# Soft-MoE attention on one core: six-pair logits blocks, a longer warm-up and small fill products in the last chain

## The chip, the cores and the metric

The kernel runs on one core of a Trainium2 chip. The metric is device time of one execution in microseconds (us), as the median of three runs. A profiled execution gives, beside its own time, a trace of each engine: TensorE (PE, with its weight loads PEld), VectorE (DVE), ScalarE (ACT), GpSimd (POOL) and the queue of SyncE (SP), which issues all DMAs of this kernel.

## What is computed

Attention with a sigmoid in place of the softmax is followed by a mixture of experts with soft routing (8 experts, 4 slots each), all in fp32:

```python
scores = scale * q @ k.T - log(S)            # 8 batches, 12 heads, S = 448, head size 64
x = sigmoid(scores) @ v                      # then x: 3584 x 768
logits = x @ phi                             # 3584 x 32
d = softmax(logits over the 3584 tokens)     # slot_input = d.T @ x : 32 x 768
h = relu(slot_input[e] @ w1[e])              # per expert, F = 1024
slot_out[e] = h @ w2[e]
c = softmax(logits over the 32 slots)
out = c @ slot_out                           # 3584 x 768
```

## The kernel before

Two heads make a pair (128 partitions), six pairs a batch, 48 pairs in all. The attention runs in 24 iterations `n` of the loop at L427, two pairs (`pa`, `pb`) each, so three iterations make a batch. The order of the instructions on PE, SP, DVE and ACT is written out by hand; every engine works through its own list in order and waits by semaphore. In an iteration PE runs `qk_full` of both pairs (L176), `av_full` of `pa` and of `pb` (L195), then `qk_mid` for the next iteration (L187) and `av_mid` (L204). DVE copies the sums of an iteration out of PSUM at the beginning of the next (`evac`, L213) into a tile `x0` or `x1`, in turn.

The logits of a pair are four products with 32 output columns (`logits_job`, L224), each into a column group of its own: with fp32, eight instructions for a pair. Before the change every iteration from the second on computes the logits of the two pairs of the iteration before it, 16 instructions in PSUM, and `logits_add` copies or adds them into `lt_all` on DVE. In the first iteration of a batch (`edge`) this stands between the two `av_full` and completes the batch before; the softmax over the tokens follows it on DVE and ACT. In the second (`after`) `spread` sends the softmax weights through DRAM: one DMA out (`zd`, L292) and four back (`dr`, L295), and `slot_mm` (L318) multiplies them with the transposed x (`y`); its products come in four groups `a` for each block `c` of 32 tokens, four products of two instructions each in a group, and group `a` reads partitions 32a and up, and so what the a-th of the four DMAs brings.

The last iteration (L461 to L479) has no next one: the partial logits of the last batch in `lt_all` are put back in PSUM by a product with the identity (L465), the pairs that are missing are added, and `last_job` does the softmax with the maximum over tokens and the slot sums in one chain. In its pauses `warm(2)` (L355) runs products nobody reads.

Weights come as 128 units of 384 KB: 64 of w1, 64 of w2. The first 50 (`N_A`) go to tiles `wa` of their own during the attention. Then, behind the last loads of v in SP's list, 18 (`N_B`) go to tiles `wb`, which lie where the attention's tiles lay: each waits until the tiles under it are free. In order of address these are the q/k tiles and their splits, `v0`, `att4`, `x0`, `att3`, `v2`, `att0` to `att2`, `v1`, a gap, `y` with `dr`, and `x1`. `wb` 0 to 14 end where `y` begins; the last three lie over `y` and wait for the last `slot_mm`. All later units and the output tiles go round the ring of these 68 tiles, each when its last reader is done: w1 products (L535), w2 products (L601), output products (L578) and their copies (L583), stores (L592).

At the start, while q and k come in, 37 small products (32x32 weights, 8 columns, L415) and three large ones (128x128, L417) run on a zeroed tile `acc`; `qk_mid(0)` follows.

Of the kernel before, what the change touches and what calls it, by code (L numbers as in the profile page):

```python
# [9 lines left out]
F32 = mybir.dt.float32  # L10
# [14 lines left out]
NFC = F // P  # L25
HALF = DM // 2
UNIT = 768
GAP = 128
N_A = 50
N_B = 18  # L30
N_LATE = 16
N_MIX = 4
QW = 2 * S
NP = B * NPR
NG = B * NQ
WARM = 3
FILL = 37
WN = 128
CW = 256
NBK = 4  # L40
# [8 lines left out]
def soft_moe_attention(ctx: ExitStack, tc: tile.TileContext, qk, v, phi, w1, w2, cst, out):  # L49
# [16 lines left out]
    acc = small.tile([P, DM], F32, name="acc")  # L66
    phi_t = small.tile([P, 256], F32, name="phit")
    phi_sb = phi_t[:, 0:NKC * NSLOT].rearrange("p (k s) -> p k s", k=NKC)
    nc.vector.memset(acc[:, 0:256], 0.0)
    nc.vector.memset(nbias, -math.log(S))  # L70
    nc.gpsimd.memset(lt_all, NEG)

    units = [("w1", e, 2 * uu + y, kh) for e in range(E) for uu in range(2) for kh in range(2) for y in range(2)]
    units += [("w2", hf, e, g, y) for hf in range(2) for e in range(E) for g in range(2) for y in range(2)]
# [42 lines left out]
    with ExitStack() as actx:  # L117
        ldq = actx.enter_context(tc.tile_pool(name="ldq", bufs=2))
        sp = actx.enter_context(tc.tile_pool(name="sp", bufs=2))
        one = {}  # L120
        for name in ("v0", "att4", "x0", "att3", "v2", "att0", "att1", "att2", "v1", "gap"):
            one[name] = actx.enter_context(tc.tile_pool(name=f"{name}p", bufs=1))
        yp = actx.enter_context(tc.tile_pool(name="yp", bufs=1))
        one["x1"] = actx.enter_context(tc.tile_pool(name="x1p", bufs=1))
        one["gap"].tile([P, GAP], F32, name="gap")
        bounce = actx.enter_context(tc.tile_pool(name="bounce", bufs=2, space=bass.MemoryType.DRAM))
        ps = actx.enter_context(tc.tile_pool(name="ps", bufs=1, space=PSUM))

        def bank2(i):
            return ps.tile([P, 2, 512], F32, name=f"b{i}")  # L130
# [73 lines left out]
                    nc.tensor.matmul(avs["p", 2 * n + i][d, 0:S], vt[r, 0, d], att[r, h, :], start=start, stop=stop)  # L204

        def new_x(n):
            xTs[n] = one[f"x{n % 2}"].tile([P, 2, S], F32, name=f"x{n % 2}")
            for i in range(2):
                xTs["p", 2 * n + i] = xTs[n][:, i, :]

# [10 lines left out]
        def logits_job(lp, pairs, first=True, last=True):  # L221
            for m, p in enumerate(pairs):
                for j in reversed(range(4)):
                    nc.tensor.matmul(  # L224
                        lp[32 * j:32 * j + 32, 0:TOK[j]], phi_sb[:, p % NPR, :],
                        xTs["p", p][:, TOF[j]:TOF[j] + TOK[j]],
                        start=(first and m == 0), stop=(last and m == len(pairs) - 1))

        def logits_add(lp, b, first):
            for r, w in ((slice(0, 64), TOK[0]), (slice(64, 128), TOK[3])):  # L230
                dst, part = lt_all[r, b, 0:w], lp[r, 0:w]
                if first:
                    nc.vector.tensor_copy(dst, part)
                else:
                    nc.vector.tensor_tensor(out=dst, in0=part, in1=dst, op=ALU.add)

        def logits(n, i):
            lp = bank2(i)[:, 0, :]
            logits_job(lp, (2 * n, 2 * n + 1))
            return lp  # L240

        def softmax_a(b):
            t1 = small.tile([P, 2, 132], F32, name="t1")
# [100 lines left out]
        def last_job(b, lg):  # L344
            t1 = small.tile([P, 2, 132], F32, name="t1")
            pe = t1[:, 0, 0:P]
            sw, sw2 = t1[:, 1, 0:NSLOT], t1[:, 1, 64:64 + NSLOT]
            m1 = small.tile([P, 2], F32, name="m1")
            cw = small.tile([P, 8], F32, name="cw")
            pa = bank2(1)  # L350
            pw = bank2(3)[:, 0, :]

            def warm(n):
                for _ in range(n):
                    nc.tensor.matmul(pw[:, 0:P], ident, ident, start=True, stop=True)  # L355

            nc.vector.tensor_reduce(out=m1[:, 0:1], in_=lg, axis=AX.X, op=ALU.max)
            nc.vector.tensor_scalar(cw[:, 0:1], m1[:, 0:1], mz[:, 0:1], -1.0, op0=ALU.max, op1=ALU.mult)
            nc.vector.tensor_tensor(out=m1[:, 1:2], in0=m1[:, 0:1], in1=mz[:, 0:1], op=ALU.max)
            nc.scalar.activation(pe, lg, AF.Exp, bias=cw[:, 0:1])  # L360
            nc.scalar.activation(cw[:, 1:2], mz[:, 0:1], AF.Exp, bias=cw[:, 0:1])
            warm(2)
            nc.tensor.matmul(pa[0:1, 0, 0:P], m1[:, 1:2], ident, start=True, stop=True)
            warm(2)
            pr = fan_out(b, pe)
            mrow = small.tile([1, 1, NSLOT], F32, name="mrow")
            nc.vector.tensor_reduce(
                out=mrow[:], in_=pa[0:1, 0, 0:P].rearrange("o (j s) -> o s j", j=4), axis=AX.X, op=ALU.max)
            fan_in(b, pr)
            for j in range(4):  # L370
                nc.tensor.matmul(pa[32 * j:32 * j + 32, 1, 0:1], mrow[:, 0, :], csb[0:1, 0:1], start=True, stop=True)
            sl = slot_mm(b, (2, 3))
            nc.vector.tensor_tensor(out=cw[:, 2:3], in0=m1[:, 1:2], in1=pa[:, 1, 0:1], op=ALU.subtract)
            nc.scalar.activation(cw[:, 3:4], cw[:, 2:3], AF.Exp)
            nc.vector.tensor_scalar(sw, sel4, cw[:, 3:4], None, op0=ALU.mult)
            nc.vector.tensor_scalar(sw2, sw, cw[:, 1:2], None, op0=ALU.mult)
            fresh = xTs[NG - 1].rearrange("p z n -> p (z n)")[:, 0:DM]
            for g, copy in enumerate((nc.scalar.copy, nc.vector.tensor_copy)):
                copy(fresh.rearrange("p (g a x) -> p g a x", g=2, a=2)[:, g], new_of(sl, g))
            pt = bank2(1)[:, 0, 0:NKC * BLK]  # L380
            for i, (part, w) in enumerate(((acc, sw2), (fresh, sw))):
                for a in range(4):
                    nc.tensor.matmul(  # L383
                        pt[32 * a:32 * a + 32, :], w, part[:, a * NKC * BLK:(a + 1) * NKC * BLK],
                        start=(i == 0), stop=(i == 1))
            nc.vector.transpose(sT[:].rearrange("p k s -> p (k s)"), pt)  # L386
            nc.scalar.copy(lt_all[:, b], lg)
            nc.vector.tensor_reduce(out=cw[:, 4:5], in_=pe, axis=AX.X, op=ALU.add)
            nc.vector.scalar_tensor_tensor(
                out=cw[:, 5:6], in0=mz[:, 1:2], scalar=cw[:, 1:2], in1=cw[:, 4:5], op0=ALU.mult, op1=ALU.add)  # L390
            nc.vector.tensor_tensor(out=cw[:, 6:7], in0=cw[:, 5:6], in1=cw[:, 3:4], op=ALU.mult)


            def finish(pool):
                pz = pool.tile([P, 2, 512], F32, name="px")[:, 0, :]
                nc.tensor.matmul(pz[:, 0:1], rep, cw[:, 6:7], start=True, stop=True)
                nc.vector.tensor_scalar(rz[:], pz[:, 0:1], 1e-9, None, op0=ALU.add)
                nc.vector.reciprocal(rz[:], rz[:])

            return finish  # L400
# [9 lines left out]
        nc.sync.dma_start(csb[:], cst)  # L410
        nc.sync.dma_start(phi_sb, phi)
        pw = bank2(0)[:, 0, :]
        for i in range(FILL):
            r = slice(i % 4 * 32, i % 4 * 32 + 32)
            nc.tensor.matmul(pw[r, 0:8], acc[r, 0:32], acc[r, 0:8], start=True, stop=True)  # L415
        for _ in range(WARM):
            nc.tensor.matmul(pw[:, 0:WN], acc[:, 0:P], acc[:, 0:WN], start=True, stop=True)  # L417
        dmy = one["att2"].tile([P, 2, S], F32, name="att2")
# [8 lines left out]
        for n in range(NG):  # L427
# [33 lines left out]
            if final:  # L461
                avs["p", pa] = bank2(2)[:, 0, :]
                av_full(pa, True, False)
                lg = bank2(0)[:, 0, 0:P]
                nc.tensor.matmul(lg, ident, lt_all[:, B - 1], start=True, stop=False)  # L465
                logits_job(lg, [NP - 4, NP - 3], first=False, last=False)
                avs["p", pb] = bank2(3)[:, 0, :]
                av_mid(n, ((False, True), (True, False)))
                new_x(n)
                xa, xb = xTs["p", pa], xTs["p", pb]  # L470
                nc.vector.tensor_copy(xa, avs["p", pa][:, 0:S])
                turn(pa)
                av_full(pb, False, True)
                logits_job(lg, [pa], first=False, last=False)
                nc.scalar.copy(xb[:, 256:S], avs["p", pb][:, 256:S])
                nc.vector.tensor_copy(xb[:, 0:256], avs["p", pb][:, 0:256])
                logits_job(lg, [pb], first=False)
                turn(pb)
                break  # L479
# [2 lines left out]
                avs["p", pa + i] = avs[n][:, i, :]  # L482
            av_full(pa, True, False)
            if edge:
                lp = logits(n - 1, 3)
                logits_add(lp, bp, False)
                softmax_a(bp)
                softmax_b(bp)
            av_full(pb, True, False)
            if n > 0 and not edge:  # L490
                lp = logits(n - 1, 3 if after else 0)
                if after:
                    combine_b(bp)
                logits_add(lp, n // NQ, n % NQ == 1)
            if after:
                slot_job(bp)
            qk_mid(n + 1)
# [96 lines left out]
    def warm(n):  # L594
        for _ in range(n):
            nc.tensor.matmul(wt[:, 0:P], ident, ident, start=True, stop=True)
# [82 lines left out]
```

## Time and profile before

| | us |
|---|---|
| median of 3 runs (lowest, highest) | 392.69 (391.61, 393.25) |
| the profiled execution | 390.81 |
| its span, first to last instruction | 389.0 |
| PE busy in the span | 364.2 |
| DVE, ACT, POOL busy | 226.5, 190.2, 3.3 |
| DMA | 97.54 MB, mean 251 GB/s |

The profile gives start and duration of each instruction, and for idle time the event that ended it. fp32 products appear as two instructions each. The span is cut here at about 284 us: before, it is attention, and after, weights and output. The profiled execution is 1.88 us below the median of the runs.

### The profile page before, as it was taken

How to read it: one execution, taken by the hardware profiler on the slowest of the kernel's cores; microseconds unless marked ns; L12 is line 12 of the kernel's file. 1: busy time of each engine (PE TensorE's matmuls, PEld its weight loads, DVE VectorE, ACT ScalarE, POOL GpSimd, SP SyncE). 2: the span in 40 equal slices, each digit the busy share in tenths (PEclk: the TensorE clock that was granted, in tenths of full speed). 3: DMA queues.
4: the chain of work that ended last, by engine and by line, in shares of the span. 5: the costliest groups of instructions: out<-in, count | busy, mean ns of one | idle time of the engine just before them, and what ended most of it. 6: DMA issues, size and time to landing. Idle time of an engine off the chain costs nothing.

```text
span 389.0 us, 9831 instructions
## 1 busy us (share of the span) xinstructions
PE 364.2 (94%) x4058; PEld 188.8 (49%) x4058; DVE 226.5 (58%) x518; ACT 190.2 (49%) x243; POOL 3.3 (1%) x13
## 2 busy tenths in 40 slices
PE   8999999999999999999999999999989989977750
PEld 5444556554555654555554456555455543313210
DVE  3555776776887677697667777776643410420340
ACT  4656675664667456566645666564530110320240
POOL 1000000000000000000000000000020000000000
PEclk9999999999999999999999999999999999999995
DMA  7777856773784567477547755442899999999987
GB/s 212 256 245 238 285 156 192 244 255 102 244 296 144 183 227 239 161 240 244 195 137 227 274 159 203 142 150 70 294 390 387 401 399 402 383 385 374 366 287 242
DMA packets 49276, 97.54 MB, mean 251 GB/s; under 512 B 5584, under 2 KB 26704, under 8 KB 49232
## 3 DMA queue, kind: packets, MB, share of 16 engines
q1 hardware_dynamic: 49232, 96.92, 72.7%
q8 instruction: 32, 0.52, 0.6%
q14 instruction: 12, 0.10, 0.1%
HBM read 85.43 MB, written 11.47 MB: 249 GB/s over the span
## 4 chain that ended last, share of the span: by engine, by line
PE 85%; DMA 9%; DVE 2%; ACT 1%; issue 1%; SPq 0%; ACTq 0%
PE b L195 29%; PE b L176 24%; PE b L187 6%; PE px L535 6%; PE b L204 5%; DMA wb<-in_w_dram 4%; PE b L318 4%; DMA wa<-in_w_dram 3%; PE b L224 3%; PE po L601 3%; PE px L578 2%; PE px L552 1%; DMA qkt<-in_qk_dram 1%; DVE wa L583 1%; PE b L383 0%
## 5 line engine op out<-in xcount | busy, mean ns | idle before, releaser
L164 ACT ACTIVATE att<-b,nbias 128x896 f32<-128x896 f32 x168 | 158.6, 1007 | 84.7 <-PE b L187 64.7
L195 PE MATMUL b<-att,v 128*64 128x448 f32 x576 | 115.3, 545 | 0.0
L176 PE MATMUL b<-qs,ks 64*128 64x448 f32 x864 | 95.7, 372 | 0.0
L176 PEld LDWEIGHTS b<-qs,ks 64*128 64x128 f32 x864 | 77.4, 184 | 26.3 <-PE b L187 6.3
L195 PEld LDWEIGHTS b<-att,v 128*64 128x64 f32 x576 | 38.5, 136 | 61.6 <-issue 54.1
L213 DVE COPY x<-b 128x896 f32<-128x896 f32 x23 | 25.1, 1091 | 33.1 <-PE b L204 33.1
L155 DVE TENSOR_TENSOR qs<-qkt,qs 128x448 fp32r<-128x448 f32 x48 | 30.0, 625 | 1.7
L155 DVE TENSOR_TENSOR ks<-qkt,ks 128x384 fp32r<-128x384 f32 x48 | 26.8, 558 | 1.6
L219 DVE STREAM_TRANSPOSE y<-x 128x448 f32<-128x448 f32 x48 | 27.3, 617 | 0.4
L187 PE MATMUL b<-qkt 64*64 64x448 f32 x192 | 25.2, 569 | 0.3 <-DMA qkt<-in_qk_dram 0.2
L153 DVE CAST qs<-qkt 128x448 fp32r<-128x448 f32 x48 | 18.4, 384 | 9.6 <-DMA qkt<-in_qk_dram 6.5
L204 PE MATMUL b<-att,v 64*64 64x448 f32 x192 | 22.4, 537 | 0.0
L583 DVE COPY wa<-px 96x768 f32<-96x768 f32 x13 | 12.2, 952 | 13.2 <-PE px L578 13.2
L583 ACT COPY wa<-px 128x768 f32<-128x768 f32 x13 | 10.3, 799 | 17.6 <-PE px L578 14.2
L535 PE MATMUL px<-wa,sT 128*32 128x256 f32 x300 | 17.8, 381 | 0.6 <-DVE sT L386 0.6
L578 PE MATMUL px<-st,lt_all 32*128 32x384 f32 (+1 forms) x128 | 16.8, 524 | 1.5 <-DVE st L614 0.7
L318 PE MATMUL b<-y,dr 32*32 32x192 f32 x896 | 17.7, 331 | 0.2 <-ACT dr L309 0.2
L224 PEld LDWEIGHTS b<-x,phit 128*32 128x32 f32 x384 | 9.1, 109 | 17.0 <-issue 11.3
L153 DVE CAST ks<-qkt 128x384 fp32r<-128x384 f32 x47 | 16.6, 353 | 0.0
L224 PE MATMUL b<-x,phit 128*32 128x96 f32 (+1 forms) x384 | 16.0, 266 | 0.2
L614 DVE COPY st<-px 128x384 f32<-128x384 f32 x2 | 1.1, 557 | 25.4 <-PE px L612 25.4
L318 PEld LDWEIGHTS b<-y,dr 32*32 32x32 f32 x896 | 12.9, 103 | 3.4 <-issue 1.4
(131 smaller groups left out, 211.5 us busy)
## 6 DMA issues: line engine op xcount, KB each, us to landing
wa<-in_w_dram SPq DMA_DIRECT2D x98, 384.0 KB, 7.0
qkt<-in_qk_dram SPq DMA_DIRECT2D x48, 448.0 KB, 4.1
wb<-in_w_dram SPq DMA_DIRECT2D x30, 384.0 KB, 5.8
v<-in_v_dram SPq DMA_DIRECT2D x48, 192.0 KB, 2.5
out_dram<-wa SPq DMA_DIRECT2D x26, 192.0 KB, 3.4
out_dram<-wa SPq DMA_DIRECT2D x26, 144.0 KB, 3.2
dr<-zd SPq DMA_DIRECT2D x28, 64.0 KB, 2.0
v<-in_v_dram SPq DMA_DIRECT2D x24, 64.0 KB, 4.2
```

The lines of the kernel that those rows point to most:

```text
L153: copy(dst[:, 0, :], src)
L155: nc.vector.tensor_tensor(out=dst[:, 1, :], in0=src, in1=dst[:, 0, :].bitcast(F32), op=ALU.subtract)
L164: nc.scalar.activation(att[:], sc[:, :, 0:S], AF.Sigmoid, bias=nbias, scale=QSCALE)
L176: nc.tensor.matmul(sc[:, h, 0:S], ks[r, z, c * P:(c + 1) * P], qs[r, y, :], start=(z + y == 0), stop=(z == 1))
L187: nc.tensor.matmul(sc[r, h, 0:S], t[d, S + NQK:QW], t[d, 0:S], start=True, stop=True)
L195: nc.tensor.matmul(avs["p", p][r, 0:S], vs[n, i][:, c, r], atts[p, c][:, h, :], start=(start and c == 0), stop=(stop and c == NFULL - 1))
L204: nc.tensor.matmul(avs["p", 2 * n + i][d, 0:S], vt[r, 0, d], att[r, h, :], start=start, stop=stop)
L219: nc.vector.transpose(ys[b][:, hp, :], xTs["p", p])
L224: nc.tensor.matmul(lp[32 * j:32 * j + 32, 0:TOK[j]], phi_sb[:, p % NPR, :], xTs["p", p][:, TOF[j]:TOF[j] + TOK[j]], start=(first and m == ...
L318: nc.tensor.matmul(sl[a // 2][32 * j:32 * j + 32, a % 2, 0:NPR * BLK], drs[b][32 * a:32 * a + 32, j, c * BLK:(c + 1) * BLK], y[32 * a:32 * ...
L535: nc.tensor.matmul(ph[32 * j:32 * j + 32, uu, 0:256], sT[:, 3 * kh + kc, :], utile[("w1", e, 2 * uu + j // 2, kh)][:, kc * 256:(kc + 1) * ...
L583: (nc.scalar.copy if g == 0 else nc.vector.tensor_copy)(ov, pf[g][0:n, :, 0:HALF])
```

## The change

- Logits: one job of six pairs (48 instructions) in the `edge` iteration, for the whole batch before; none in the other iterations. `logits_add` becomes a plain copy. The last batch's first four pairs are done in one job in the last iteration, on top of `lt_all[:, B - 1]`, which POOL sets to zero at the start.
- So x of three iterations must live: `x0`, `x1` (now beside `x0`) and `x2` (now last in the address order). To make room the gap goes, and `N_A` falls to 49, while `N_B` rises to 19: the total of 68 tiles stays, and `wb` 0 to 15 now end where `y` begins.
- The start has 40 small products and eight large ones, and the clearing of `acc` is split, so that its first 32 columns, all that the small ones read, are cleared first.
- Each of the two `warm(2)` of the last chain becomes `warm(1)` and 13 small products.

```diff
-N_A = 50
-N_B = 18
+N_A = 49
+N_B = 19
-WARM = 3
-FILL = 37
+WARM = 8
+FILL = 40
+CHAIN = 13
...
-    nc.vector.memset(acc[:, 0:256], 0.0)
+    nc.vector.memset(acc[:, 0:32], 0.0)
+    nc.vector.memset(acc[:, 32:256], 0.0)
     nc.vector.memset(nbias, -math.log(S))
     nc.gpsimd.memset(lt_all, NEG)
+    for r, w in ((slice(0, 64), TOK[0]), (slice(64, 128), TOK[3])):
+        nc.gpsimd.memset(lt_all[r, B - 1, 0:w], 0.0)
...
-        for name in ("v0", "att4", "x0", "att3", "v2", "att0", "att1", "att2", "v1", "gap"):
+        for name in ("v0", "att4", "x0", "x1", "att3", "v2", "att0", "att1", "att2", "v1"):
             one[name] = actx.enter_context(tc.tile_pool(name=f"{name}p", bufs=1))
         yp = actx.enter_context(tc.tile_pool(name="yp", bufs=1))
-        one["x1"] = actx.enter_context(tc.tile_pool(name="x1p", bufs=1))
-        one["gap"].tile([P, GAP], F32, name="gap")
+        one["x2"] = actx.enter_context(tc.tile_pool(name="x2p", bufs=1))
...
-            xTs[n] = one[f"x{n % 2}"].tile([P, 2, S], F32, name=f"x{n % 2}")
+            xTs[n] = one[f"x{n % NQ}"].tile([P, 2, S], F32, name=f"x{n % NQ}")
...
-            warm(2)
+            warm(1)
+            fill(CHAIN, pw, ident)
             nc.tensor.matmul(pa[0:1, 0, 0:P], m1[:, 1:2], ident, start=True, stop=True)
-            warm(2)
+            warm(1)
+            fill(CHAIN, pw, ident)
             pr = fan_out(b, pe)
...
-        for i in range(FILL):
-            r = slice(i % 4 * 32, i % 4 * 32 + 32)
-            nc.tensor.matmul(pw[r, 0:8], acc[r, 0:32], acc[r, 0:8], start=True, stop=True)
+        def fill(n, dst, src):
+            for i in range(n):
+                r = slice(i % 4 * 32, i % 4 * 32 + 32)
+                nc.tensor.matmul(dst[r, 0:8], src[r, 0:32], src[r, 0:8], start=True, stop=True)
+        fill(FILL, pw, acc)
...
-                logits_job(lg, [NP - 4, NP - 3], first=False, last=False)
+                logits_job(lg, range(NP - NPR, NP - 2), first=False, last=False)
...
             if edge:
-                lp = logits(n - 1, 3)
-                logits_add(lp, bp, False)
+                lp = bank2(3)[:, 0, :]
+                logits_job(lp, range(2 * (n - NQ), 2 * n))
+                logits_copy(lp, bp)
                 softmax_a(bp)
                 softmax_b(bp)
             av_full(pb, True, False)
-            if n > 0 and not edge:
-                lp = logits(n - 1, 3 if after else 0)
-                if after:
-                    combine_b(bp)
-                logits_add(lp, n // NQ, n % NQ == 1)
+            if after:
+                combine_b(bp)
             if after:
                 slot_job(bp)
```

## Rows read from the trace of the kernel before

**Rows 1.** The page, span in forty slices: granted clock in tenths, DMA busy in tenths.
```profile
PEclk9999999999999999999999999999999999999995
DMA  7777856773784567477547755442899999999987
```

**Rows 2.** Windows of the end: stretch, busy us (instructions) per engine, clock, DMA share, GB/s.
```profile
272.00:284.00 12.00, 11.72 (x103) 5.90 (x100) 7.68 (x19) 7.53 (x10) 0.00 (x0) 1.00 0.89 296
284.00:288.00 4.00, 3.82 (x134) 2.88 (x133) 1.44 (x6) 1.00 (x5) 0.31 (x1) 1.00 1.02 408
288.00:340.00 52.00, 49.93 (x669) 23.80 (x668) 15.19 (x36) 7.94 (x24) 1.86 (x7) 1.00 1.03 394
```

**Rows 3.** SP's queue: start us, us, line, DMA, count; then its waits, us in total.
```profile
271.68 17.81 SPq L93 DMA_DIRECT2D wb<-in_w_dram  x18
...
SPq L145 <- PE b L204: 3.7, 1, 3.7
SPq L93 <- PE b L318: 3.5, 1, 3.5
```

**Rows 4.** Weight loads of PE that waited, 325 to 365 us: us in total, times, longest.
```profile
PEld po L601 <- DMA wb<-in_w_dram: 8.6, 9, 2.0
```

**Rows 5.** The chain that ended last: start us, us, what (a third iteration, then an `edge`).
```profile
31.94 4.66 PE b L195 x24
...
42.75 2.41 PE b L195 x12
45.15 0.57 PE b L224 x14
```

**Rows 6.** Timeline: spread and logits of the first four batches; last, the second's landings.
```profile
55.71 1.75 SPq L295 DMA_DIRECT2D dr<-zd  x4
58.31 0.38 PEld L224 LDWEIGHTS b<-x,phit 128*32 128x32 f32 x16 [0.70 <-issue]
...
90.56 1.75 SPq L295 DMA_DIRECT2D dr<-zd  x4
93.03 0.38 PEld L224 LDWEIGHTS b<-x,phit 128*32 128x32 f32 x16 [0.70 <-issue]
...
125.08 1.75 SPq L295 DMA_DIRECT2D dr<-zd  x4
127.83 0.38 PEld L224 LDWEIGHTS b<-x,phit 128*32 128x32 f32 x16 [0.70 <-issue]
...
158.77 1.75 SPq L295 DMA_DIRECT2D dr<-zd  x4
162.55 0.38 PEld L224 LDWEIGHTS b<-x,phit 128*32 128x32 f32 x16 [0.70 <-issue]
...
DMA to landing us min/median/max: 1.8/2.0/2.1
```

**Rows 7.** Timeline of the start: start us, us, engine, line, op, count, idle before.
```profile
1.18 1.23 PE L415 MATMUL b<-acc 32*32 32x8 f32 x74 [1.18 <-DVE nbias L70]
2.35 1.65 PE L417 MATMUL b<-acc 128*128 128x128 f32 x6
4.16 1.67 PE L187 MATMUL b<-qkt 64*64 64x448 f32 x4 [0.17 <-DMA qkt<-in_qk_dram]
5.98 0.97 PE L187 MATMUL b<-qkt 64*64 64x448 f32 x4
```

**Rows 8.** Timeline of the last chain.
```profile
267.37 2.20 PE L318 MATMUL b<-y,dr 32*32 32x192 f32 x112
283.71 0.15 DVE L359 TENSOR_TENSOR m<-m,mz 128x1 f32<-128x1 f32 x1
284.23 0.71 PE L355 MATMUL b<-csb 128*128 128x128 f32 x4
284.28 0.31 DVE L299 STREAM_TRANSPOSE phit<-t 128x128 f32<-128x128 f32 x1 [0.42 <-ACT t L360]
284.87 0.62 PE L303 MATMUL b<-phit,csb 32*128 32x128 f32 x8
```

More of the change, by code (lines that the diff above doesn't have):

```diff
@@ L27 @@
 UNIT = 768
-GAP = 128
-N_A = 50
-N_B = 18
+N_A = 49
+N_B = 19
 N_LATE = 16
@@ L227, in logits_job, with logits_copy @@
                         start=(first and m == 0), stop=(last and m == len(pairs) - 1))
-        def logits_add(lp, b, first):
+        def logits_copy(lp, b):
             for r, w in ((slice(0, 64), TOK[0]), (slice(64, 128), TOK[3])):
[L231 to L240, printed above, removed]
+                nc.vector.tensor_copy(lt_all[r, b, 0:w], lp[r, 0:w])
         def softmax_a(b):
```

## The prediction

> **What bounds the kernel now.** I read the slices of the page first: the granted clock is full until the last slice, and the DMA engines go from six to eight tenths busy to nine and more at about 284 us and stay there [rows 1]. So there are two stages with two limits. Then the chain of waits. Up to 280 us nearly all of it is PE, one block behind the other without a gap: two `av_full` 4.66 us, or with the `edge` logits between them 2.41 us, 0.57 us, and so on [rows 5]. In this stage a microsecond that PE saves is a microsecond saved, for ACT and DVE are about half idle and the q/k loads come long before use.
>
> In the second stage the chain names PE too, and that misleads. The windows show the DMA engines at a share of 0.89 or more from 272 us on, and at 1.03 with 394 GB/s from 288 to 340 us [rows 2]. From 340 us PE's weight loads wait nine times for a weight that has not landed, 8.6 us in total [rows 4], and the output can't begin before the last of them. The reader should count units of 384 KB (0.393 MB). SP starts the `wb` loads at 271.68 us; before, it stood 3.7 us for `av_mid` of iteration 22, which frees the tile of the last small v load [rows 3]. By 284 us 12 us at 296 GB/s have brought 9.0 units, by 288 us another 4 us at 408 GB/s have brought 4.2, 13.2 in all. Fifteen were issued by then, as many as end below `y`, and SP then waited 3.5 us for the last `slot_mm` [rows 3]. So when that wait ended some 1.8 units were still under way, and the engines never ran dry. From 272 us on the end is the beginning of this stream plus its bytes over its rate. What moves it is when SP gets to `wb` 0, and how many units are left then.
>
> **The change part by part.** *Logits.* A block of two pairs costs 0.57 us [rows 5]. How that grows with pairs no row shows for logits, but `av_full` does: 24 products take 4.66 us and 12 take 2.41 [rows 5], so twelve more cost 2.25 us, 0.1875 us each, and since two run side by side in two column groups, 0.375 us pass for 448 columns, 0.107 for 128. A pair's eight logits instructions run four side by side, so a pair takes 2 x 0.107 = 0.214 us, and the block's fixed part is 0.57 - 0.43 = 0.14 us (`av_full` gives 2.41 - 2.25 = 0.16, about the same). Six pairs: 0.14 + 6 x 0.214 = 1.42 us. Bounds for a pair: 0.19 us, if the first pair carries part of the fixed cost, and 0.285 us, half of a block, if nothing is shared. I take 0.214, which comes from the longer stream. Until `av_mid` of iteration 22 the change takes out 22 blocks, 12.54 us, and puts in seven, 9.94 us: -2.6 us (with 0.19 for a pair -3.2, with 0.285 only -0.6). The blocks stand where the edge block stood, so no new split of `av_full` arises. The last iteration pays two pairs more, 0.43 us, behind `wb` 0.
>
> DVE loses two small operations in two of three iterations, off the path, nothing gained. The third x tile takes one wait away that no row shows as a wait, nothing again. The clearing on POOL is done hundreds of microseconds before its reader.
>
> *What is late next.* In the `after` iteration `slot_mm` now begins where the logits began, 0.57 us sooner, but its data do not: `spread` hangs on DVE and two DMA trips. In the second batch the four copies are issued from 90.56 to 92.31, so the fourth at about 91.88, and land 2.0 us later, at 93.9 [rows 6]. `slot_mm` would begin at 93.03, and the first product of group 3 is its 25th instruction; at the pace of 112 in 2.20 us [rows 8], some 17 ns each after the first, it is due at 93.44. PE waits 0.44 us. The same reading of the first batch: copy issued at 57.03, landed at 59.0, due at 58.72, a wait of 0.2; of the third: 126.40, 128.35, due at 128.24, a wait of 0.1 [rows 6]. In the other four batches the copies come about a microsecond earlier beside the logits, in the fourth at 162.1 for 162.96 [rows 6]: no wait. Sum 0.75 us (between 0, if the DMA trips run ahead as the iterations get shorter, and 1.5, if other batches follow). PE's waits are so short that I expect no loss of clock.
>
> *Start.* The end of it is set by the second q/k load: the second half of `qk_mid(0)` starts at 5.98 us, just behind it [rows 7]. Sixteen instead of six large instructions now stand ahead of the first half. The clock's column says full here, but six take 1.65 us, 0.25 apart, where four of the same kind take 0.71 in the last chain [rows 7, 8], so they ran at half pace, 1.2 GHz, and by 5.98 `qk_mid` had the other level: 1.67 us for its first half, 0.97 for the second. Small products begin about 0.2 us sooner (split clearing) and 80 take 1.25 us at the pace of 74 in 1.16, to about 2.2. Sixteen at 0.25 end at 6.4 if the pace stays, near 5.9 if the clock rises when `qk_mid`'s first half saw it, near 5.5 if it rises with the first large ones. `qk_mid` then does both halves side by side in the 0.91 us of its later iterations. So the cost is 0 to 0.5 us, up to 1.2 if the clock rises late; I take 0.15.
>
> *One unit more.* The units in front of `y` stay 65 (50 + 15 before, 49 + 16 after) and the tiles under `wb` are free at the same events, but one unit fewer is in when SP gets to `wb` 0, and the stream behind carries 79 instead of 78. At 394 to 408 GB/s [rows 2] that is 0.98 us. Bounds: 0, if the stream in its slower part (296 GB/s) waits for issues and not for bandwidth, and 1.33 at that rate. The backlog of 1.8 units at 288 us speaks for bandwidth, so I take 0.98.
>
> *Last chain.* The second pause is on PE's path: the transposed weights are ready at 284.59, but PE is at its idle products until `fan_out` at 284.87 [rows 8]. `warm(1)` takes half of 0.71 us, some 0.32, and 26 small instructions 0.41 us at the start's pace of 15.7 ns: 284.23 + 0.73 = 284.96, +0.1 us; at twice that pace -0.1. The first pause has the same length and ends about when the maximum is there (283.86): nothing. I take +0.05. The Trainium skill, page "TensorE: Matmul & The Clock Gate", section "Wait — 56ns, not 53.3ns?", says that products never start closer than about 25 ns, however small. The row has 74 in 1.16 us, 15.7 ns, so here the measurement decides; by the page's figure the pause would last 0.65 us and the chain would lose 0.3 us instead of 0.05. Either way, like the 0.43 us of the last logits, it lies behind `wb` 0 and moves the release of `y` only: the stream has 1.8 units, 1.8 us of work, under way there. Cost nothing; without that cover 0.5 us.
>
> **Sum.** `wb` 0 moves by -2.6 + 0.75 + 0.15 = -1.7 us; with the unit the end moves by -0.7 us. The profiled execution would go from 390.81 to 390.1 us. It lies 1.88 us below the median of the runs; I carry the difference over to the median: 392.69 - 0.7 = 392.0 us.
>
> **Rivals.** *The unit is free.* The slow 296 GB/s of 272 to 284 us speaks for a stream that could take more; the full share of 288 to 340 us against it [rows 2]. Then -1.7 us, 391.0.
>
> *The block does not get shorter.* If six pairs cost three blocks of two, 1.71 us, only the moved block is saved: -0.57 + 0.75 + 0.15 + 0.98 = +1.3 us, 394.0. The stream of `av_full` speaks against it.
>
> *The clock falls in the last chain (slower).* Small products instead of large ones, with pauses between, may not hold the 2.4 GHz level. If PE fell to 1.2 GHz at about 284 us and stayed there until the w1 products have run 10 us, `fan_out` and `slot_mm`, 0.6 and 2.2 us [rows 8], would double, +2.8 us, and the w1 products, PE being busy nearly all the time from 288 us on [rows 2], would fall back 5 us. Of these 7.8 us the stream covers 4.8, with 1.8 units under way and three over `y`; then it waits for tiles of the ring that PE has not freed. 3.0 us idle: -0.7 + 3.0 = +2.3 us, 395.0. It decides from the granted clock between 284 and 300 us, and from 4.8 us of delay on. The slices show no fall before in spite of idle times there [rows 1]. The Trainium skill's page on TensorE's clock gate, section "A second HAM failure mode: psum-queue depth-cycling", describes such swings where PE idles briefly between groups of products; the slices show none before the last, when PE's work is over.
>
> **How the numbers follow.** Forecast 392.0 (391.0 to 393.2 by its terms): 0.52. Unit free, 391.0 (390.2 to 391.6): 0.20. Block not shorter, 394.0: 0.10. Clock, 395.0 (394 to 398): 0.08. Left over, mostly copies that are not late and a cheaper pair with the unit free, near 390: 0.10. The range that leaves out the clock and half of the left over is 389.9 to 394.2. About 0.5%, 1.96 us, can be told from no change: below 390.7 lie most of the left over and a part of the second case, 0.22; above 394.7 the clock and a little of the third, 0.11; between, 0.67.
>
> **What would show it.** Right: logits blocks of about 1.42 us, seven of them; PE waiting for `dr` in the first batches; `wb` 0 issued near 270.0 us; DMA share 1.0 from there on, and the last weight products waiting for DMA as before. Wrong: `wb` 0 near 269 (copies in time), near 272 (blocks no shorter or a cold start), a clock below full at 284 to 300 us, or an end that moves by as much as `wb` 0 does.

## The result and the profile after

The changed kernel takes 393.65 us (median; 391.69 to 395.52) beside 391.48 us for the kernel before on the same chip: 1.0048 times as long, with an interval of 1.0031 to 1.0064. Some 2 us were lost where 0.7 us were forecast to be gained. The profiled execution took 391.69 us, its span is 389.9 us against 389.0. It is the fastest of the 22 runs of the changed kernel, so the traces show 0.9 us of a loss that is 2.2 us in the medians. One profiled execution below (a_pad32) ran at a granted clock of 0.56 and took 596.12 us; it enters no comparison. In what follows, before and after are the two kernels, and `after` in code letters is the iteration of that name.

The front of the kernel did what was forecast of it, and more. The lines show first the block of six pairs in the chain that ended last (start, us, what), then SP's queue at the first `wb` load (start, us, line, count).

```profile
43.87 1.45 PE b L226 x42
```
```profile
269.00 6.24 SPq L96 DMA_DIRECT2D wb<-in_w_dram  x7
```

A block costs 1.45 us (forecast 1.42), and SP gets to `wb` 0 at 269.00 instead of 271.68 [rows 3], 2.68 us sooner. No wait for the `dr` copies stands in this trace. So 2.7 us were in hand at 269 us in this execution, and they were all gone, with 0.9 more, at the end.

Where they went is in the last chain. The timeline of PE (start, us, line, op, shape, count, idle before and what ended it):

```profile
282.40 0.41 PE L412 MATMUL b<-csb 32*32 32x8 f32 x26
282.74 0.63 PE L296 MATMUL b<-phit,csb 32*128 32x128 f32 x8
283.30 0.24 PE L366 MATMUL b<-csb,mrow 1*32 1x1 f32 x8
283.70 1.92 PE L311 MATMUL b<-y,dr 32*32 32x192 f32 x90 [0.17 <-ACT dr L302]
287.83 0.81 PE L311 MATMUL b<-y,dr 32*32 32x192 f32 x22 [2.21 <-issue]
```

In the middle of the last `slot_mm`, after 90 of its 112 instructions, PE stands still for 2.21 us, and "issue" says that it waited for nothing that the profile shows: all the data were there. SP's wait for this `slot_mm` is 6.1 us, 3.5 before [rows 3]:

```profile
SPq L96 <- PE b L311: 6.1, 1, 6.1
```

The windows after it (stretch, busy us and instructions of PE, PEld, DVE, ACT, POOL, clock, DMA share, GB/s) show the price:

```profile
272.00:284.00 12.00, 11.67 (x180) 5.56 (x187) 5.97 (x18) 5.80 (x11) 0.32 (x1) 1.00 0.97 345
286.00:288.00 2.00, 0.17 (x11) 0.17 (x20) 0.00 (x0) 0.00 (x0) 0.00 (x0) 1.00 0.96 375
288.00:290.00 2.00, 2.00 (x38) 0.83 (x22) 0.56 (x1) 0.65 (x2) 0.59 (x3) 0.68 0.33 97
290.00:292.00 2.00, 1.42 (x15) 0.71 (x17) 0.93 (x4) 0.00 (x0) 1.28 (x5) 0.50 0.87 303
288.00:300.00 12.00, 11.42 (x184) 6.22 (x172) 3.41 (x10) 1.06 (x4) 1.87 (x7) 0.86 0.83 286
```

From 288 to 290 us the weight stream runs dry, 97 GB/s; `y` comes free too late for its three units. In the kernel before, the same view has 386 GB/s from 288 to 300 us:

```profile
288.00:300.00 12.00, 11.14 (x179) 6.16 (x178) 3.41 (x10) 1.06 (x4) 1.86 (x7) 1.00 1.01 386
```

100 GB/s less for 12 us are 1.2 MB or 3.0 units, about 3.0 us of a stream at 400 GB/s. With the 2.7 us won at `wb` 0 that comes to +0.3 us; the span has +0.9. The granted clock drops too: it is 0.50, the 1.2 GHz level, from 288.7 to 292.1 us (0.68 is the mean of a stretch with both levels). PE has been idle before, from 285.6 to 287.8 us, and over the idle stretch itself the clock is still 1.00.

### The profile page after: what moved, and what is told of

It reads as the page before. It is cut to its first block, busy times and chain, and to the rows that moved or that the text cites. A ratio compares the mean times of both kernels' runs of the same rounds, so it can differ in the third digit from the quotient of the medians.

```text
span 389.9 us, 9935 instructions
## 1 busy us (share of the span) xinstructions
PE 364.4 (93%) x4122; PEld 192.0 (49%) x4122; DVE 219.0 (56%) x489; ACT 190.2 (49%) x243; POOL 3.7 (1%) x15
## 4 chain that ended last, share of the span: by engine, by line
PE 78%; DMA 16%; DVE 1%; issue 1%; ACT 1%; SPq 0%; ACTq 0%
PE b L197 29%; PE b L178 24%; DMA wa<-in_w_dram 10%; DMA wb<-in_w_dram 6%; PE b L189 6%; PE b L206 5%; PE b L311 5%; PE b L226 3%; PE px L532 2%; PE px L575 2%; PE b L416 1%; DVE wa L580 1%; PE b L412 0%; PE b L378 0%; PE px L609 0%
## 5 line engine op out<-in xcount | busy, mean ns | idle before, releaser
L189 PE MATMUL b<-qkt 64*64 64x448 f32 x192 | 23.6, 562 | 0.0
L333 DVE SCALAR_TENSOR_TENSOR acc<-acc,t,b 128x384 f32<-128x384 f32 x12 | 6.8, 611 | 17.6 <-PE b L311 17.6
L554 ACT COPY hh<-px 128x32 f32<-128x32 f32 x8 | 1.5, 185 | 24.5 <-PE px L549 24.5
```

The source lines that it names most:

```text
L189: nc.tensor.matmul(sc[r, h, 0:S], t[d, S + NQK:QW], t[d, 0:S], start=True, stop=True)
```

## The experiments

The first theory: PE's instructions come by DMA in blocks, and the stop is a block that is not there yet. For this speaks section 3 of the page (queue, packets, MB, share of 16 engines):

```profile
q8 instruction: 32, 0.52, 0.5%
```

After has 8,244 weight loads and products on PE (counted in the trace), before 8,116: about 258 for each of the 32 packets, so a block would be about 128 pairs of a weight load and a product. An fp32 product is two such pairs; the counts below are in pairs, and "products" in a line of the timeline means one of each pair. The Trainium skill, "Runtime: NRT & Kernel Launch", section "Instruction fetch mechanics", gives 256 instructions for a block and calls the cost of crossing one mostly hidden. The 256 agree; the 2.21 us here, if it is this, are not hidden, and the runs decide.

Theory A (blocks; the expectations call it the fetch theory): the stop shifts along the program with the number of instructions ahead of it. Theory B (a consequence of the small products): it goes with them. Theory C: clock, the slower rival of the prediction. The expectations also name a stream theory: the loss comes from the unit more behind `wb` 0 and the moved tiles. Each run has a name, in brackets; a number such as 0.9982 is its time over that of before on the same chip, with a 95% interval.

**The large warm-up products of the last chain put back, in both pauses** (a_warm2; 16 pairs more than before ahead of the last `slot_mm`, in place of 64).
```diff
-            warm(1)
-            fill(CHAIN, pw, ident)
+            warm(2)
```


> The changed kernel with warm(2) twice in the last chain, as before: 48 fewer small product pairs (96 PE instructions) ahead of the last slot_mm. Fetch theory: the 2.21 us in which PE stood still inside the last slot_mm of the changed kernel, with no releaser, is a late block of PE instructions (the page counts 32 instruction packets on queue q8 for 8244 loads and products, some 258 each, so a block edge comes every 256 or so), and the edge now lies 96 instructions later, in the first w1 products: no idle of over 0.3 us inside slot_mm, an idle of about 1 us in the first 24 w1 products instead, wb behind y issued near 285.7 us, full clock at 288 to 292 us, time ratio to before 0.995 to 0.999. Stream theory (the loss comes from one weight unit more behind wb 0 and from the moved tiles, and the idle in slot_mm belongs to the slot products themselves): idle of about 2 us in slot_mm again, ratio 1.003 to 1.006.


Measured: 0.9982 [0.9947, 1.0017], 391.2 us for 391.64. `slot_mm` runs in one piece. The stop is still there, among the w1 products: with 48 pairs fewer ahead it comes 47 products later, the 22 that were left of `slot_mm`, 16 of L376 and 9 of L530.

```profile
283.75 2.35 PE L311 MATMUL b<-y,dr 32*32 32x192 f32 x112 [0.18 <-ACT dr L302]
...
290.48 1.07 PE L530 MATMUL px<-wa,sT 128*32 128x256 f32 x15 [1.83 <-issue]
```

So it does not belong to `slot_mm` or to the small products. `y` is free by then, and the stream is not held up for it.

**64 small products in iteration 1 of after** (a_pad64), some 250 us ahead.
```diff
+            if n == 1:
+                fill(64, bank2(0)[:, 0, :], ident)
```


> The changed kernel with 64 small products more (nobody reads them) in iteration 1 of the attention, some 220 us ahead of the last chain, so that together with the 64 pairs that the change added the count ahead of the last slot_mm is 256 instructions over that of before: the block edges lie where they lay before. Fetch theory: the 2.21 us idle in slot_mm is gone although only work was added; an idle of about 0.3 us at the rz product like before (291.63 there); wb 0 about 1 us later than in the changed kernel (64 x 16 ns), near 270.0; time ratio to before 0.996 to 1.000, so faster than the changed kernel. Stream theory: the idle in slot_mm stays, and the added work comes on top: ratio 1.006 to 1.008.


Measured: 1.0112 [1.006, 1.0165]. I had counted 64 pairs; each fp32 product is two, so it was 128, a whole block by A, and the stop is where it was, within one product:

```profile
285.90 1.92 PE L311 MATMUL b<-y,dr 32*32 32x192 f32 x91 [0.17 <-ACT dr L302]
289.92 0.67 PE L311 MATMUL b<-y,dr 32*32 32x192 f32 x21 [2.10 <-issue]
```

The expectation missed, by my count, but a shift by one block that leaves the stop in place is what A wants.

**32 of them** (a_pad32 for the times, a_pad32b, the same kernel, for the trace), 64 pairs, or 128 above before.
```diff
+            if n == 1:
+                fill(32, bank2(0)[:, 0, :], ident)
```


> As the kernel with 64 small products in iteration 1, but with 32. Each fp32 product is two load and product pairs, so 64 of them were 128 pairs, one whole block of 256 instructions, and the stop stayed where it was in slot_mm; 32 are 64 pairs, half a block, which with the 64 pairs of the change puts the edges where they lie before. Fetch theory: no idle in the last slot_mm, 0.3 to 1 us without a releaser near the rz product instead; wb 0 about 1.0 us later than in the changed kernel, near 270.0; ratio to before 0.997 to 1.001, faster than the changed kernel (1.0048) although it does more. Stream theory: the idle in slot_mm stays and the ratio is 1.005 to 1.009.

> The kernel with 32 small products in iteration 1 again, for a look at an undisturbed execution. Fetch theory: slot_mm in one piece of about 2.35 us, 0.3 to 1 us without a releaser at the rz product, wb 0 near 270.0 us. Stream theory: about 2 us idle in slot_mm.


Measured: 1.0014 [0.9981, 1.0047] in place of 1.0048, with more work than after. The lines are the last `slot_mm`, in the trace of a_pad32b, and the idle time without a releaser that is left behind it:

```profile
286.12 2.35 PE L311 MATMUL b<-y,dr 32*32 32x192 f32 x112 [0.17 <-ACT dr L302]
```
```profile
PE px L391 <- issue: 0.6, 1, 0.6
```

32 products which nobody reads, 250 us earlier, take the stop out of `slot_mm`. B and C have no room for that.

**The small products of the chain alone, in the kernel before** (b_fill13; 48 pairs).
```diff
-            warm(2)
+            warm(1)
+            fill(13, pw, ident)
```
(in both pauses, and the loop over small products as a function `fill`.)


> The kernel before with nothing but warm(1) and 13 small products in place of each warm(2) of the last chain: 48 pairs, 96 instructions more ahead of the last slot_mm. Fetch theory: a block edge falls into the last quarter of slot_mm, about 104 of its 112 products in, and PE stands still there for 2 to 3 us with no releaser; the stores' and weights' stream runs dry for 1 to 2 us near 290 us; ratio 1.004 to 1.009, about as slow as the whole change. Stream theory: the chain gets 0 to 0.2 us longer behind a stream that covers it: ratio 0.999 to 1.001.


Measured: 1.0115 [1.0061, 1.0169], 396.37 us for 391.64, from four runs. This edit alone costs 4.7 us, more than A's expectation of up to 0.9%. The stop comes 17 products later than in after with 16 pairs fewer ahead:

```profile
287.01 2.17 PE L318 MATMUL b<-y,dr 32*32 32x192 f32 x107 [0.17 <-ACT dr L309]
291.44 0.85 PE L318 MATMUL b<-y,dr 32*32 32x192 f32 x5 [2.26 <-issue]
```

**The block of six pairs alone: after with the old start and the old chain** (a_logits; the same count as before).
```diff
-WARM = 8
-FILL = 40
+WARM = 3
+FILL = 37
...
-    nc.vector.memset(acc[:, 0:32], 0.0)
-    nc.vector.memset(acc[:, 32:256], 0.0)
+    nc.vector.memset(acc[:, 0:256], 0.0)
...
-            warm(1)
-            fill(CHAIN, pw, ident)
+            warm(2)
```


> The changed kernel with the start and the last chain of before, so the logits blocks, the third x tile and the 49 + 19 weight tiles alone: the count of PE instructions ahead of the last slot_mm is that of before. Fetch theory: no idle in slot_mm, about 0.3 us at the rz product as before; wb 0 2.2 to 2.7 us earlier than before; the end earlier by that less 0 to 1.3 us for the unit: ratio 0.994 to 0.998. Stream theory: the loss is in this part: ratio 1.003 to 1.006.


Measured: 0.9955 [0.9925, 0.9985], 389.78 us for 391.64, -1.9 us; `wb` 0 at 269.29. The logits are a gain, as forecast, and a part of it reaches the end: in the two traces 2.4 us are won at `wb` 0, and the spans, 387.8 and 389.0 us, differ by 1.2.

**The engines emptied: a store of 64 KB of the last slot sums ahead of the `wb` loads in SP's list** (a_hold), so that no weight moves while the chain runs. The instructions on PE are after's, all 64 pairs too many.
```diff
+            hold = bounce.tile([P, P], F32, name="zd")
+            nc.sync.dma_start(hold[:], fresh[:, 0:P])
```


> The changed kernel with one small store in front of the wb loads in SP's list that reads the slot sums, so that no weight is under way during the last chain; the result of the store is used by nothing. Fetch theory: the block of PE's instructions is late because it queues behind the weights, so with empty DMA engines the 2.21 us idle in slot_mm shrinks to under 0.5 us, and slot_mm takes about 2.2 us in one piece; the whole kernel is some 10 to 16 us slower, since the weights begin at 288 us. Rivals: if the idle comes from PE itself (its pace, the clock, the small products), or if fetching a block takes that long on empty engines too, about 2 us of idle stay.


Measured: 405.21 us in its one run, the price of a stream that begins at 287.08 us. No stop:

```profile
284.03 2.36 PE L311 MATMUL b<-y,dr 32*32 32x192 f32 x112 [0.17 <-ACT dr L302]
```

The DMA views by queue show one instruction packet each, in a_hold from 282.5 to 283.5 us, ahead of `slot_mm`, and in after from 284.5 to 285.5 us, in the midst of it:

```profile
q8 instruction: 1, 0.02, 5.7%
```
```profile
q1 hardware_dynamic: 146, 0.40, 101.3%
q8 instruction: 1, 0.02, 7.0%
```

In after PE goes on only at 287.83. So the stop needs both: a block edge at this place, and DMA engines that are full of weights.

The traces hold start and end of every such packet, 16,384 bytes each, and they show the delay itself. "Pair 3,254" is the 3,254th product instruction of PE from the start of the trace; the third column is the time at which PE starts the pair 128 before the one in the last column.

| kernel | weights in transit | PE 128 pairs before, us | packet starts | packet ends | pair at the edge starts |
|---|---|---|---|---|---|
| a_hold | no | 282.75 | 283.01 | 283.93 | 3,254 at 285.54, no stop |
| after | yes | 282.45 | 285.27 | 286.39 | 3,255 at 287.83, after the stop |
| a_warm2 | yes | 283.97 | 287.88 | 288.95 | 3,254 at 290.48, after the stop |
| b_fill13 | yes | 285.89 | 288.91 | 289.98 | 3,256 at 291.44, after the stop |
| before | yes | 286.25 | 289.51 | 290.60 | 3,254 at 291.91, after 0.28 us |
| a_edge (below) | yes | 284.98 | 288.32 | 289.40 | 3,254 at 291.56, no stop |

The packet itself takes about 1 us with and without weights. What differs is its start: 0.3 us after the pair in the third column without weights, 2.8 to 3.9 us after it with them. In all ten traces with a stop PE goes on 1.2 to 1.6 us after the end of a packet. In a_edge and the three other kernels without a stop beside weights PE comes to the edge 1.5 to 2.2 us after the packet's end, so the block is there.

**Moved by choice: the large products in the chain, and 15 small ones at the start** (a_edge; 34 pairs fewer than before), and the same again with more runs (a_edge_r).
```diff
-FILL = 40
+FILL = 15
...
-            warm(1)
-            fill(CHAIN, pw, ident)
+            warm(2)
```


> The logits blocks and tiles of the changed kernel, warm(2) twice in the last chain, and a start of 15 small and eight large products: 34 pairs fewer ahead of the last slot_mm than in the kernel before. Fetch theory: the edges move back by 34 pairs, one to the middle of the last slot_mm, whose block was asked for long before, the next some 128 pairs on into the w1 products, by when over 6 us have passed: no idle without a releaser between 280 and 300 us (under 0.3 us), ratio 0.990 to 0.995, below the 0.9955 of the kernel with the logits part alone. Stream theory: the position of the edges does not matter, ratio as with the logits part alone, 0.995 to 0.997; a start with fewer small products might cost up to 0.5 us.

> The fastest kernel so far again (logits part, warm(2) twice, 15 small and eight large products at the start), beside the one before on the same chip. If the place of the edges and the fuller start are worth what they seemed: ratio 0.990 to 0.994. If its first result was luck: 0.995 to 0.997, as with the logits part alone.


Measured: 0.9923 [0.9894, 0.9952] and 0.9951 [0.9923, 0.9980]: 389.19 us for 391.76, and 390.42 us for 392.21. Neither trace has an idle of PE without a releaser from `slot_mm` to the first w1 products. This version is faster than both kernels; against a_logits the intervals overlap, and the repeat lies at the edge of what was forecast for luck, so a gain over a_logits is not shown.

**The old start, with fewer small products** (both 34 pairs fewer): in a_logits (a_edge3) and in before (b_edge).
```diff
-FILL = 37
+FILL = 20
```


> The logits blocks and tiles alone, with the start of before (three large products) cut to 20 small ones: 34 pairs fewer than before, so the block edges lie as in the kernel with 15 small and eight large products. Fetch theory: no idle without a releaser between 280 and 300 us, ratio 0.990 to 0.995, like that kernel's 0.9923. If the eight large products are what helped there, 0.995 to 0.998.

> The kernel before with 20 instead of 37 small products at the start, nothing else: 34 pairs fewer, the block edges as in the fastest kernel so far. Fetch theory: the 0.28 us (0.9 in another execution) without a releaser at the rz product is gone; it lies behind y and is covered for the most part by the stream, so ratio 0.997 to 1.001. If the edge is what made the fastest kernel fast, and not the logits: 0.992 to 0.996.


Measured: 0.9964 [0.9937, 0.9991] and 1.0024 [0.9997, 1.0051]. No stop in either trace, and no gain beside a_logits and before, where a stop of 0.3 to 0.9 us at the `rz` product remains; both times missed the fetch theory's ranges, 0.990 to 0.995 and 0.997 to 1.001. That the small stop costs nothing is not shown by it, for the shorter start has a price of its own in these two traces: the first `av_full` begins at 12.33 us in a_edge3 (10.58 in a_logits) and at 11.64 in b_edge (10.82 in before). The first `qk_full`, in a_logits and in a_edge3:

```profile
6.64 3.92 PE L177 MATMUL b<-qs,ks 64*128 64x448 f32 x36
```
```profile
7.30 5.11 PE L177 MATMUL b<-qs,ks 64*128 64x448 f32 x36
```

**The start alone, in before** (b_start), and **49 units in front, 19 behind, alone** (b_unit).
```diff
-WARM = 3
-FILL = 37
+WARM = 8
+FILL = 32
...
-    nc.vector.memset(acc[:, 0:256], 0.0)
+    nc.vector.memset(acc[:, 0:32], 0.0)
+    nc.vector.memset(acc[:, 32:256], 0.0)
```
```diff
-GAP = 128
-N_A = 50
-N_B = 18
+GAP = 896
+N_A = 49
+N_B = 19
```


> The kernel before with the eight large products and the split clearing at the start, and 32 small products, so that the count of PE instructions ahead of the last slot_mm is that of before. Both theories: what the longer start is worth by itself. The prediction took +0.15 us, 0 to 0.5: ratio 0.999 to 1.0015. If the large products bring the clock up sooner, the first blocks run at full pace: up to 0.4 us sooner, ratio 0.999. No idle in slot_mm either way.

> The kernel before with 49 + 19 weight tiles instead of 50 + 18 (the gap in front of y grows by the 768 columns, so that 16 wb tiles end where y begins), nothing else: one unit more behind wb 0, the count of PE instructions unchanged. If the stream behind wb 0 is bound by bandwidth, as the prediction took it: +0.98 us, ratio 1.002 to 1.0035. If the unit is carried in slack: ratio 0.999 to 1.001. Fetch theory: no new idle of PE in slot_mm in either case, but the idle at the rz product may grow, since the weight stream is denser.


Measured: 0.9999 [0.998, 1.0018] and 0.9993 [0.997, 1.0015]. Neither costs anything that can be told.

**The small products of the chain kept, the count made equal to before** (a_same; after with `FILL = 8`).
```diff
-FILL = 40
+FILL = 8
```


> The whole change, small products in the last chain included, but with eight instead of 40 small products at the start: the count of PE instructions ahead of the last slot_mm is that of before again, and no work is added. Fetch theory: the 26 small products cost nothing by themselves; slot_mm in one piece, 0.3 to 1 us without a releaser at the rz product, ratio 0.993 to 0.998 like the logits part alone. If the small products cost time in the chain by themselves (their pace, a falling clock): idle or a clock below full between 281 and 292 us, ratio 1.000 to 1.005 like the whole change.


Measured: 1.0004 [0.9973, 1.0035]. `slot_mm` is in one piece again, with the 26 small products in front of it:

```profile
286.43 2.35 PE L311 MATMUL b<-y,dr 32*32 32x192 f32 x112 [0.17 <-ACT dr L302]
```
```profile
PE px L391 <- issue: 0.7, 1, 0.7
```

That is the sharpest line between A and B, and A has the place of the stop. It does not have the time: 1.0004 lies in the range of the rival, in which the small products cost time by themselves, and the gain of a_logits is not here. The trace puts the loss in front of the chain: `wb` 0 comes at 271.72, 2.4 us later than in a_logits, while from `wb` 0 to the end a_same takes 118.1 us and a_logits 118.5. The clock is full from 281 to 292 us.

Laid side by side, by the number of load and product pairs that stand ahead of the last `slot_mm`, against before (read from each trace):

| kernel | pairs | where PE stands without a releaser | us |
|---|---|---|---|
| a_edge, a_edge_r, a_edge3, b_edge | -34 | nowhere | 0 |
| before, a_logits, a_same, b_unit, b_start | 0 | `rz` product, behind 24 or more w1 products | 0.3 to 0.9 |
| a_warm2 | +16 | after 9 w1 products | 1.83 |
| b_fill13 | +48 | `slot_mm`, after 107 of 112 | 2.26 |
| after | +64 | `slot_mm`, after 90 | 2.21 |
| a_pad32b | +128 | `rz` product | 0.6 |
| a_pad64 | +192 | `slot_mm`, after 91 | 2.10 |
| a_hold (no weights in transit) | +64 | nowhere | 0 |

From one row to the next the stop moves by as many instructions as were added, and after 128 pairs it is back. Counted from the start of the program it does not move at all: PE goes on with pair 3,254, 3,255 or 3,256 in every kernel with a stop but the two padded ones, and in those with 3,382 (a_pad32b) and 3,384 (a_pad64), one block further. It is the only place in each whole trace where PE's products stand without a releaser. That the stop is a late block of instructions is shown by its place, its period, its independence of what the instructions are, the packet that ends just ahead of its end in each trace, and its absence when the engines are empty. When the packet is asked for is not in the trace. If that is when PE enters the block before, the last 128 pairs ahead of the edge last 2.9 us in after, and the block comes 5.4 us after it was asked for; in a_hold the packet was done 1.2 us after.

## Why the prediction was wrong

**What bounds the kernel** held in part. A stream that runs dry costs time, as the result shows. But the end does not simply follow the start of the `wb` stream: in b_edge, with before's bytes, `wb` 0 comes 1.56 us later than in before (273.24 for 271.68), and the span is the same, 389.0 us. From `wb` 0 to the end the kernels of the change (a_hold aside) take 117.4 to 118.8 us without a stop of over 1 us, 119.9 in a_warm2, 120.9 in after and 121.8 in a_pad64; those of before's kind take 115.8 to 117.3, and b_fill13 122.7. What else sets the end was not tested.

**The logits term** held: 1.45 us a block against 1.42, -2.68 us at `wb` 0 in the profiled execution against -2.6 before the other terms (2.4 in a_logits), and -1.9 us of time in a_logits. The rival "the block does not get shorter" falls with it.

**The `dr` wait**, +0.75 us, was no constant. After's trace has none; a_edge_r and a_same show one in the waits up to 270 us (us in total, times, longest), the first with `wb` 0 at 271.00:

```profile
PEld b L311 <- DMA dr<-zd: 1.7, 5, 0.6
```
```profile
PEld b L311 <- DMA dr<-zd: 1.2, 5, 0.3
```

The bounds, 0 to 1.5 us, were about right, with 1.7 a little above. (By the prediction's own figures the first batch's wait is 0.3 us and not 0.2.) The wait comes in some executions and not in others, and not only with the change: b_edge has 0.7 us of it. It explains a part of where `wb` 0 comes in the changed kernels, between 269.0 and 271.7 us; in a_edge3 it is 0.3 us, and the late start makes 271.36.

**The start**, +0.15 us: `qk_mid(0)` ran both halves in 0.98 us from 5.66 us on, and `qk_full` began at 6.57 us, 0.4 us ahead of the end of `qk_mid` before [rows 7]; with b_start at 0.9999, no cost that can be told, as bounded.

```profile
0.95 1.25 PE L412 MATMUL b<-acc 32*32 32x8 f32 x80 [0.95 <-DVE acc L69]
2.13 3.60 PE L416 MATMUL b<-acc 128*128 128x128 f32 x16
5.66 0.98 PE L189 MATMUL b<-qkt 64*64 64x448 f32 x8
```

**One unit more**, +0.98 us, was too dear in the kernel before: b_unit gives -1.2 to +0.6 us, as the rival "unit is free" says. In the changed kernel this is not settled, since a_logits loses 1.2 us of what it won at `wb` 0. The stream could take more in spite of its full share: at 288 to 300 us b_unit moves 402 GB/s where before moves 386, both at a share of 1.01 or more:

```profile
288.00:300.00 12.00, 10.55 (x194) 5.89 (x175) 3.41 (x10) 1.06 (x4) 1.86 (x7) 1.00 1.03 402
```

I took the share for the bandwidth, where the GB/s of the two windows [rows 2] had already differed by 14 at shares of 1.02 and 1.03.

**The last chain**, "cost nothing", is the step that failed, and it turned the sign. The pace of the small products was right: 26 take 0.34 us from start to next start, and the second pause lasts 1.07 us up to `fan_out` where it lasted 0.95, +0.12 us for a forecast of +0.1. They count 48 pairs more, though, and with 16 at the start that puts a block edge into `slot_mm`, where PE takes a pair every 20 ns or less, while the DMA engines are full. The prediction priced these products by their pace alone and had no wait of PE for its own instructions. With it the chain is 2.21 us longer, more than the cover of 1.8 us, which the stream's earlier start makes smaller still: 3.0 us of stream were lost. In b_fill13, without the logits, the same edit costs 4.7 us.

**The slower rival** forecast a clock that falls in the chain, 3 us of an idle stream and 395.0 us. The fall is there, from 288.7 to 292.1 us, and so are the 3 us. But the order is another: the clock stood at 1.00 through the chain and the stop, and fell behind it. It fell there in the three traces with a stop in `slot_mm` (after, a_pad64, b_fill13) and in none of the others that are compared here, a_warm2 with its 1.83 us included. a_same keeps the small products and has this `slot_mm` at full pace. The loss of 2.2 us comes near to the rival's 2.3, for a reason that it did not name. The fall has a share in the price: 24 w1 products take 2.17 us in after and 1.50 in before, and from the last `wb` issue to the next load 2.5 us pass instead of 1.5, so about 1 us by estimate. No run has the stop in `slot_mm` without the fall.

**In sum:** 0.7 us were forecast as gain. That 393.65 us lies in the stated range, 389.9 to 394.2, is luck: the range was drawn around a gain, from a median of 392.69 of three runs, where 22 runs gave 391.48. In the traces `wb` 0 comes 2.7 us sooner, and from there to the end after takes 120.9 us where before takes 117.3 and a_logits 118.5. So 2.4 of the 3.6 us lost come with the stop and the fall of the clock behind it, and 1.2 are there without them. What stays open: the median lost 2.2 us, and only the fastest execution of after was profiled, so where the other 1.3 us go is not known; a `wb` 0 as late as in other traces, 271 us and more, could be the reason. a_same has no long stop and still no gain (1.0004 against 0.9955 of a_logits). It differs from a_logits by the start and by the 26 small products; in its profiled execution it starts late and waits for `dr`, but whether this is so in its other executions, these runs don't tell. Nor is it settled whether a_edge is faster than a_logits at all.

## What to carry to other kernels

Before adding or removing instructions on PE, even idle ones at the start, look for idle time with "issue" as its releaser in bursts of short products that run beside a full DMA load: its place is set by the count of all instructions ahead of it, and some tens of idle products added or removed far away move it out of a stretch on which something waits. The packets of the instruction queue (q8 here) tell whether it is a late block: PE went on 1.2 to 1.6 us after one had ended. When an edit's own cost is nothing and the time still moves, compare where these stops lie in the two traces first. Read a stream's slack from its GB/s in comparable windows, not from the DMA share. And before a trace is taken as the account of a median, look where its own time lies among the runs.

## What was not expected of the hardware

A stop of 1.8 to 2.3 us on PE with all its data there, tied to the number of instructions, back after one block of 128 pairs, and gone in the one run without a DMA load. The Trainium skill's sentence on blocks that are "mostly hidden" ("Runtime: NRT & Kernel Launch", section "Instruction fetch mechanics") holds for all of the 32 or 33 blocks of a trace but one at most. At that one, with DMA engines full of weights, it did not hold.

And one and the same start takes different times from execution to execution: the first eight products of `qk_mid`, behind 80 small and 16 large instructions that are the same in each, took 0.98 us in after, 0.98 in a_warm2, 1.05 in a_hold, 1.82 in a_pad64 and 1.86 in a_pad32b, and `qk_full` began between 6.57 and 7.63 us. With before's start it began between 6.64 (a_logits) and 7.06 us (b_unit). The trace's first entry for the granted clock, at 1.00, also comes at different times: at 5.40 us in after, 5.43 in a_logits, 7.69 in a_pad32b and 9.85 in a_edge3. A difference of 0.3 us between two starts can't be read from one trace of each.
